# GpSimd's long pooling and splitting operations cut into short chains, in a fused pooled-attention and top-1 MoE kernel

## The chip, the core and the metric

The kernel runs on one core of a Trainium2 chip. The metric is device time in microseconds (us) of one execution, the median of several runs. Engines are named as the profile names them: PE (matmul) and PEld (weight load), DVE (VectorE), ACT (ScalarE), POOL (GpSimd), SP (the engine that issues most transfers).

## The reference

Attention over keys and values that are averaged in groups of 8, then a mixture of 8 experts in which each token uses one:

```python
k_p = k.reshape(B, H, Sp, pool, D).mean(axis=3)      # B, H, S, D = 8, 8, 576, 64; pool = 8
v_p = v.reshape(B, H, Sp, pool, D).mean(axis=3)
scores = scale * np.matmul(q, k_p.transpose(0, 1, 3, 2))
attn = exp(scores - max); attn = attn / sum(attn)
x = np.matmul(attn, v_p)                             # as 4608 rows of 512
expert_idx = np.argmax(x @ w_gate, axis=1)           # 8 experts
y = np.maximum(x @ w1[e], 0.0) @ w2[e]               # e: the row's expert; w1 512 x 1024, w2 1024 x 512
out = softmax(x @ w_gate)[expert_idx] * y
```

## The kernel before

Each engine's instructions stand in the order in which the Python code calls them (a manual schedule); waits between engines are put in by the framework, and each engine takes its own queue in order.

The first part, up to about 240 us, is attention and routing. Its work is cut into 36 units of 128 query rows; `u_pt`, `u_lo`, `u_pv` and `u_nrm` are the steps of one unit: transpose the probabilities on PE, split them into two halves of 16 bits (ACT line 482, DVE line 488), multiply with the pooled V (PE line 514), normalise on DVE (lines 543 to 554). Between them stand scores of later units (`g_s` on PE, `g_min` on DVE line 466, `g_exp` on ACT line 473) and small DVE steps of routing, called fillers, one or two at a time (lines 589 to 660). A Python table, `hooks`, hangs other work on places of the loop over units: `put(16, "q", pool_k, 6, 0)` runs part 0 of pooling K of batch 6 at the start of unit 16.

POOL's queue holds, in this order and mixed by those places:
- pooling (`pool`, lines 296 to 299) of K and V of batches 1 to 7, 14 in all, written k1, v1 up to k7, v7 here. A loaded K or V is a tile of 128 partitions by 5 chunks by 512 values. Three additions halve it: 1280 values to `t1`, 640 to `t2`, 320 to `kp` or `vp`. From batch 4 on the first addition is part 0 and stands in one unit, the other two are part 1 and stand in the next. `t1` and `t2` lie in the staging tile `st2[0]`, into which SP later loads the first half of expert 0's second weight (line 88);
- scatters of routed rows (`scatter`, line 649), 36 indirect transfers of one unit's rows each; `apart` (line 567) puts two memsets between some of them;
- splits of expert 0's weights (`wsplit` with "p" or "P", lines 109 and 110): five times a product and a difference of 1024 values per partition;
- the split of the first block of routed rows (`split_early`, lines 819 and 820), from which SP makes the transposed input of the experts (line 829).

PE takes kp and vp in `k_pe` (line 326) and `v_pe` (line 340); they stand in PE's queue at fixed units, k7 at 24 and v7 at 25. ACT writes the high half of a weight (line 101), DVE the low half of three of them in quarters (line 793, `lsplit`).

The second part, from about 240 us, is a loop over blocks of 256 rows through the experts. The lines of the change are not in it.

Of the kernel before, what the change touches and what calls it, by code (L numbers as in the profile page):

```python
# [13 lines left out]
OP = mybir.AluOpType  # L14
# [18 lines left out]
def kernel(  # L33
# [10 lines left out]
    nc = tc.nc  # L44
    B, H, S, D = q.shape
    N, Dm = out.shape
# [21 lines left out]
    def walloc(pool, s):  # L68
        W1[s] = [pool.tile([128, DC, F], F16, name=f"w1_{s}{h}") for h in range(2)]
        W2[s] = [pool.tile([128, FC, Dm], F16, name=f"w2_{s}{h}") for h in range(2)]  # L70
# [21 lines left out]
    def wsplit(s, i, what="hl"):  # L92
        if i < 4:
            src = st1[i // 2][:, i % 2, :]
            h, l = W1[s][0][:, i, :], W1[s][1][:, i, :]
        else:
            i -= 4
            src = st2[i // 2][:, 2 * (i % 2):2 * (i % 2) + 2, :]
            h, l = W2[s][0][:, 2 * i:2 * i + 2, :], W2[s][1][:, 2 * i:2 * i + 2, :]
        if "h" in what:  # L100
            nc.scalar.activation(h, src, AF.Copy, scale=SW)  # L101
        if "l" in what:
            nc.vector.scalar_tensor_tensor(l, src, SW, h, op0=OP.mult, op1=OP.subtract)
        if what in "pP":
            last_pool[:] = []
            t, sw = scratch[2 * (what == "P") + i % 2], swc[:, 0:1]
            if len(src.shape) == 3:
                t, sw = t.rearrange("p (c x) -> p c x", c=2), swc[:, :, None]
            nc.gpsimd.tensor_tensor(t, src, sw.to_broadcast(list(src.shape)), op=OP.mult)
            nc.gpsimd.tensor_tensor(l, t, h, op=OP.subtract)  # L110

    jp = st1[1].rearrange("p c x -> p (c x)")[:, 0:128].bitcast(I32)
    nc.gpsimd.iota(jp, pattern=[[1, 128]], base=0, channel_multiplier=-1)
# [48 lines left out]
    zf = consts.tile([128, 1], F32, name="zf")  # L162
    swc = consts.tile([128, 2], F32, name="swc")
# [24 lines left out]
    for e in range(E):  # L188
# [13 lines left out]
    xh = bd[2].rearrange("p (j a x) -> p j a x", j=2, a=2)  # L202
    ys = [x.rearrange("p h d -> p (h d)") for x in ql]
    xg, xg2 = (VB[i].rearrange("p y c s x -> p (y c s x)").bitcast(F32)[:, 0:2 * XW]
               .rearrange("p (j x) -> p j x", j=2) for i in (2, 0))
# [37 lines left out]
    for c in range(5):  # L243
        src = w_gate.rearrange("(h d) e -> d h e", d=D)[:, HS[c]:HS[c] + 3, :]
# [45 lines left out]
    t1 = st[:, 0:1280].rearrange("p (c x) -> p c x", c=5)  # L290
    t2 = st[:, 1280:1920].rearrange("p (c x) -> p c x", c=5)

    def pool(src, dst, what=(0, 1)):
        last_pool[:] = []
        if 0 in what:
            nc.gpsimd.tensor_tensor(t1, src[:, :, 0:4 * D], src[:, :, 4 * D:], op=OP.add)  # L296
        if 1 in what:
            nc.gpsimd.tensor_tensor(t2, t1[:, :, 0:2 * D], t1[:, :, 2 * D:], op=OP.add)
            nc.gpsimd.tensor_tensor(dst, t2[:, :, 0:D], t2[:, :, D:], op=OP.add)

    def pool_now(src, dst, part):
        p1 = pbig[:, 0:1280].rearrange("p (c x) -> p c x", c=5)
# [6 lines left out]
    def pool_k(b, part):  # L309
        if part == 0:  # L310
            KVS["kp", b] = work.tile([128, 5, D], F32, name="kp", bufs=2)
        pool(kv[(2 * b) % 3], KVS["kp", b], (part,))

    def pool_v(b, part):
        if part == 0:
            KVS["vp", b] = work.tile([128, 5, D], F32, name="vp", bufs=2)
        pool(kv[(2 * b + 1) % 3], KVS["vp", b], (part,))
# [374 lines left out]
    def pooled(n, b):  # L692
        KVS[n, b] = work.tile([128, 5, D], F32, name=n, bufs=2)
        return kv[(2 * b + (n == "vp")) % 3], KVS[n, b]
# [4 lines left out]
    src, kp = pooled("kp", 0)  # L699
# [11 lines left out]
    src, vp = pooled("vp", 0)  # L711
# [83 lines left out]
    for j, at in enumerate((12, 13, 18, 17, 26, 27, 23, 28)):  # L795
        put(at, "act2", wsplit, 0, j, "h")
    for j, at, what in ((0, 14, 'P'), (2, 20, 'P'), (5, 31, 'p'), (6, 26, 'p'), (7, 30, 'p')):
        put(at, "q", wsplit, 0, j, what)
# [16 lines left out]
        pass_ids(gB, iB, gA, iA)  # L815

    def split_early():
        x = xg[:, :, 0:Dm]
        nc.gpsimd.tensor_tensor(xh[:, :, 0], x, zf[:, :, None].to_broadcast([128, 2, Dm]), op=OP.add)
        nc.gpsimd.tensor_tensor(xh[:, :, 1], x, xh[:, :, 0], op=OP.subtract)  # L820

    def split_x(x=xg, h=xh):
        x = x[:, :, 0:Dm]
# [27 lines left out]
    def first_block():  # L851
        split_early()
        keep_ids()
        move_ids()
        take_ids()
# [262 lines left out]
    for j in range(2):  # L1118
        x, h = xg[:, j, 0:Dm], xh[:, j]
# [9 lines left out]
    with tc.If(nc.values_load(tab[0:1, 1:2], engines=[ENG.Activation, ENG.DVE, ENG.SP], min_val=0, max_val=1) > 0):  # L1129
        for j in range(8):  # L1130
            wsplit(1, j)
        for j in range(4):
            wload(2, (2 * j, 2 * j + 2))
# [114 lines left out]
```

## Time and profile before

| what | value |
|---|---|
| median of 3 runs | 688.49 us (687.96 to 693.12) |
| the profiled execution | 686.63 us |
| its span, first to last instruction | 684.7 us |
| mean granted clock of TensorE | 0.937 |
| PE, DVE, ACT, POOL busy | 87%, 52%, 42%, 41% of the span |
| attention and routing | up to about 240 us |

The profiled execution lies 1.86 us under the median and 1.93 us over its own span. Busy shares are means over both parts. A DVE or POOL instruction that has started and is held by the other engine counts as busy, so a long duration of a small instruction is a wait.

### The profile page before, as it was taken

What the parts mean: (1) busy time and instruction counts of PE and PEld (TensorE: products, weight loads), DVE (VectorE), ACT (ScalarE), POOL (GpSimd) and SP (SyncE); (2) the same over time, 40 slices, a digit from 0 to 9 for tenths busy, and PEclk for the clock granted to TensorE, in tenths of its full rate; (3) what the DMA queues carried; (4) which work ended last, traced back from release to release, by engine and by line L of the source; (5) the groups of instructions that cost most, each with busy time, mean ns of one, the idle gap of its engine ahead of it and who ended that gap; (6) DMA issues with size and microseconds to landing.
All of it is one profiled execution on the core that took longest, in us unless ns stands there. A gap on an engine that the chain in (4) does not pass through costs nothing. (4 is left out here: it accounts for less than half of the span.)

```text
span 684.7 us, 16103 instructions
## 1 busy us (share of the span) xinstructions
PE 595.1 (87%) x4637; PEld 428.9 (63%) x4638; DVE 356.3 (52%) x749; ACT 288.3 (42%) x634; POOL 278.8 (41%) x488
## 2 busy tenths in 40 slices
PE   6697898688768695999699999998999899999992
PEld 4586797577756453467375666674777566667751
DVE  4659988999897423522268286222451272122121
ACT  1375777567753023412357266222542272222221
POOL 5794759776485511021224325223132223021221
PEclk9998989999999797899799999999999989999997
DMA  8974968947648561831285884923174223320200
GB/s 241 295 220 102 267 216 230 290 126 188 212 115 283 168 151 47 290 93 44 81 276 169 245 261 116 349 75 94 42 279 123 57 60 95 77 61 31 61 31 13
DMA packets 104397, 105.65 MB, mean 154 GB/s; under 512 B 62502, under 2 KB 72742, under 8 KB 104360
## 3 DMA queue, kind: packets, MB, share of 16 engines
q1 hardware_dynamic: 97720, 85.46, 45.0%
q0 software_dynamic: 6640, 19.71, 8.0%
q8 instruction: 22, 0.36, 0.2%
q14 instruction: 15, 0.12, 0.1%
HBM read 71.77 MB, written 22.06 MB: 137 GB/s over the span
## 5 line engine op out<-in xcount | busy, mean ns | idle before, releaser
L962 PEld LDWEIGHTS <-bd 128*128 128x128 f16 x936 | 93.5, 101 | 129.9 <-issue 19.0
L1143 POOL TENSOR_TENSOR spacer<-ql,iG 1x1 f32<-1x1 f32 x44 | 19.5, 443 | 207.3 <-ACT ql L1139 206.4
L825 DVE TENSOR_TENSOR bd<-vb,bd 128x1024 f16<-128x1024 f32 x21 | 25.8, 1227 | 145.8 <-ACT bd L824 88.9
L473 ACT ACTIVATE p<-ps,nmx 128x72 f32<-128x72 f32 x288 | 68.7, 325 | 53.1 <-DVE nmx L466 50.4
L956 DVE SCALAR_TENSOR_TENSOR bd<-pp,bd 128x512 f16<-128x512 f32 x44 | 30.3, 691 | 94.6 <-ACT bd L952 88.7
L952 ACT ACTIVATE bd<-pp 128x512 f16<-128x512 f32 x44 | 26.2, 597 | 113.2 <-PE pp L895 63.7
L962 PE MATMUL po<-w,bd 128*128 128x512 f16 x264 | 62.9, 398 | 4.8 <-PEq L1187 4.8
L962 PE MATMUL po<-kv,bd 128*128 128x512 f16 x264 | 60.7, 388 | 3.9 <-ACT bd L952 2.5
L456 PE MATMUL ps<-bd,qT 128*128 128x144 f32 x256 | 51.5, 331 | 9.8 <-ACT p L473 8.4
L1144 POOL DMA_INDIRECT out_dram<-ql,iG x44 | 46.5, 1058 | 22.0 <-issue 20.6
L649 POOL DMA_INDIRECT x_by_expert<-XR,rpos x36 | 35.8, 993 | 42.0 <-DVE ri L543 9.7
L962 PE MATMUL pq<-w,bd 128*128 128x512 f16 x192 | 47.9, 410 | 5.4 <-ACT qt L101 3.9
L296 POOL TENSOR_TENSOR st<-kv 128x1280 f32<-128x1280 f32 x14 | 40.8, 2914 | 25.7 <-DMA kv<-in_k_dram 18.4
L893 PE MATMUL pp<-kv,w 128*128 128x256 f16 (+2 forms) x176 | 44.4, 264 | 5.6 <-issue 5.3
L962 PE MATMUL pq<-kv,bd 128*128 128x512 f16 x216 | 48.4, 379 | 0.2 <-ACT bd L952 0.2
L456 PEld LDWEIGHTS ps<-bd,qT 128*128 128x128 f32 x256 | 40.6, 218 | 12.2 <-ACT p L473 9.7
L514 PE MATMUL po<-vb,ph 128*128 128x146 f16 (+2 forms) x384 | 33.7, 237 | 15.3 <-DVE l L552 4.9
L893 PE MATMUL pp<-kv,qt 128*128 128x256 f16 (+2 forms) x176 | 44.6, 265 | 2.0 <-issue 2.0
L1139 ACT ACTIVATE ql<-po,gB 128x512 f32<-128x512 f32 x22 | 15.1, 685 | 73.1 <-PE L893 43.4
L894 PE MATMUL ps<-kv,qt 128*128 128x256 f16 (+2 forms) x176 | 43.9, 260 | 1.4 <-issue 1.4
L895 PE MATMUL pp<-kv,qt 128*128 128x256 f16 (+2 forms) x176 | 44.6, 265 | 0.0
L894 PE MATMUL pp<-kv,qt 128*128 128x256 f16 (+2 forms) x176 | 44.6, 265 | 0.0
(219 smaller groups left out, 1430.2 us busy)
## 6 DMA issues: line engine op xcount, KB each, us to landing
st<-in_moe_w_dram SPq DMA_DIRECT2D x32, 1024.0 KB
vb<-x_by_expert SPq DMA_DIRECT2D x17, 514.0 KB
kv<-in_k_dram SPq DMA_DIRECT2D x7, 1024.0 KB
kv<-in_v_dram SPq DMA_DIRECT2D x7, 1024.0 KB
qt<-in_q_dram SPq DMA_DIRECT2D x6, 1024.0 KB
qt<-in_q_dram SPq DMA_DIRECT2D x4, 512.0 KB
kv<-in_k_dram SPq DMA_DIRECT2D x8, 128.0 KB
kv<-in_k_dram SPq DMA_DIRECT2D x2, 512.0 KB
```

The source lines that it names most:

```text
L296: nc.gpsimd.tensor_tensor(t1, src[:, :, 0:4 * D], src[:, :, 4 * D:], op=OP.add)
L456: nc.tensor.matmul(ps[:, x * 2 * KP:(x + 1) * 2 * KP], t[:, h, :], BD[b % 3][:, :, h, :], start=True, stop=True)
L473: nc.scalar.activation(p[:, h * KP:(h + 1) * KP], ps[:, x * KP:(x + 1) * KP], AF.Exp, bias=nmx[:, x:x + 1], scale=-1.0)
L514: nc.tensor.matmul(po[:, half, cols], a[:, c * 128:(c + 1) * 128], VB[b % 3][:, y, c, sl, 0:CW], start=st, stop=False, skip_group_check=True)
L649: st = nc.gpsimd.indirect_dma_start(out=xs, out_offset=bass.IndirectOffsetOnAxis(ap=Z["pos"][:, u:u + 1], axis=0), in_=X[:, u, :], in_offs ...
L893: nc.tensor.matmul(dst, wh, xT[:, d, 0:n], start=(d == 0), stop=False)
L894: nc.tensor.matmul(dst, wh, xT[:, DC + d, 0:n], start=False, stop=False)
L895: nc.tensor.matmul(dst, wl, xT[:, d, 0:n], start=False, stop=(d == DC - 1))
L952: nc.scalar.activation(hT[0][:, 2 * k:2 * k + 2, :].rearrange("p f t -> p (f t)"), pH[k], AF.Relu)
L956: V.scalar_tensor_tensor(l, pH[k], 0.0, h, op0=OP.max, op1=OP.subtract)
L962: nc.tensor.matmul(y, hT[x][:, f, 128 * j:128 * j + 128], W2[s][z][:, f, :], start=(half == x == z == f == 0), stop=(half == z == 1 and f ...
L1144: st = nc.gpsimd.indirect_dma_start(out=out, out_offset=bass.IndirectOffsetOnAxis(ap=iG[:, j:j + 1], axis=0), in_=ys[j], in_offset=None, b ...
```

## The change

Three places are rewritten; what is computed stays the same, and nothing else moves.

- `pool`: the three additions run chunk by chunk. Five chains of three additions, of 256, 128 and 64 values, take the place of one chain of 1280, 640 and 320. Part 0 is now chunks 0 and 1, part 1 chunks 2 to 4.
- `wsplit` on POOL: product and difference alternate over four quarters of 256 values, in place of one pair of 1024.
- `split_early`: copy and difference alternate over four pieces of 256 values, in place of one pair of 1024.

```diff
@@ wsplit
-            nc.gpsimd.tensor_tensor(t, src, sw.to_broadcast(list(src.shape)), op=OP.mult)
-            nc.gpsimd.tensor_tensor(l, t, h, op=OP.subtract)
+            for x in range(4):
+                c = (slice(None), slice(256 * x, 256 * x + 256))
+                if len(src.shape) == 3:
+                    c = (slice(None), x // 2, slice(256 * (x % 2), 256 * (x % 2) + 256))
+                nc.gpsimd.tensor_tensor(t[c], src[c], swc[:, 0:1].to_broadcast([128, 256]), op=OP.mult)
+                nc.gpsimd.tensor_tensor(l[c], t[c], h[c], op=OP.subtract)
@@ pool
-        if 0 in what:
-            nc.gpsimd.tensor_tensor(t1, src[:, :, 0:4 * D], src[:, :, 4 * D:], op=OP.add)
-        if 1 in what:
-            nc.gpsimd.tensor_tensor(t2, t1[:, :, 0:2 * D], t1[:, :, 2 * D:], op=OP.add)
-            nc.gpsimd.tensor_tensor(dst, t2[:, :, 0:D], t2[:, :, D:], op=OP.add)
+        for c in ((0, 1), (2, 3, 4))[what[0]] if len(what) == 1 else range(5):
+            nc.gpsimd.tensor_tensor(t1[:, c], src[:, c, 0:4 * D], src[:, c, 4 * D:], op=OP.add)
+            nc.gpsimd.tensor_tensor(t2[:, c], t1[:, c, 0:2 * D], t1[:, c, 2 * D:], op=OP.add)
+            nc.gpsimd.tensor_tensor(dst[:, c], t2[:, c, 0:D], t2[:, c, D:], op=OP.add)
@@ split_early
-        x = xg[:, :, 0:Dm]
-        nc.gpsimd.tensor_tensor(xh[:, :, 0], x, zf[:, :, None].to_broadcast([128, 2, Dm]), op=OP.add)
-        nc.gpsimd.tensor_tensor(xh[:, :, 1], x, xh[:, :, 0], op=OP.subtract)
+        for j in range(2):
+            for c in (slice(0, Dm // 2), slice(Dm // 2, Dm)):
+                nc.gpsimd.tensor_tensor(xh[:, j, 0, c], xg[:, j, c], zf.to_broadcast([128, Dm // 2]), op=OP.add)
+                nc.gpsimd.tensor_tensor(xh[:, j, 1, c], xg[:, j, c], xh[:, j, 0, c], op=OP.subtract)
```

POOL's queue at v7, the last pooling, before the change (`kv_131` is the loaded V, `st_0_66` holds t1 and t2; in brackets the semaphores for which a row waits: DMAHW a load, DMASW an earlier scatter, Pool POOL itself):

```order
L296 TENSOR_TENSOR st_0_66<-kv_131 128x1280 [waits DMAHW3_49,DMAHW2_49]
L648 MEMSET spacer 1x1 [waits Pool_49]
L649 DMA x_by_expert<-XR,rpos 38016x514 [waits DMASW7_49]
L298 TENSOR_TENSOR st_0_66<-st_0_66 128x640 [waits Pool_49]
L299 TENSOR_TENSOR vp<-st_0_66 128x320 [waits Pool_49]
```

The same place after the change, from the first addition to the first chain behind the scatter:

```order
L300 TENSOR_TENSOR st_0_66<-kv_131 128x256 [waits DMAHW3_49]
L301 TENSOR_TENSOR st_0_66<-st_0_66 128x128 [waits Pool_49]
L302 TENSOR_TENSOR vp<-st_0_66 128x64 [waits Pool_49]
L300 TENSOR_TENSOR st_0_66<-kv_131 128x256
L301 TENSOR_TENSOR st_0_66<-st_0_66 128x128 [waits Pool_49]
L302 TENSOR_TENSOR vp<-st_0_66 128x64 [waits Pool_49]
L651 MEMSET spacer 1x1
L652 DMA x_by_expert<-XR,rpos 38016x514 [waits DMASW7_49]
L300 TENSOR_TENSOR st_0_66<-kv_131 128x256
```

Two whole chains now stand ahead of the scatter and three behind it; within a chain each addition waits for POOL's own semaphore, and the first addition of a chain does not.

POOL's queue at the last product and difference ahead of `split_early`, before the change (`kv_154` is scratch, `w_01_63` the weight's low half, `bd_161` the split rows, `vb_164` the loaded block):

```order
L109 TENSOR_TENSOR kv_154<-st_1_67,swc 128x1024
L842 UNCONDITIONAL_BRANCH
L110 TENSOR_TENSOR w_01_63<-kv_154,w_00_62 128x1024 [waits Activation_49,Pool_49]
L819 TENSOR_TENSOR bd_161<-vb_164,zf 128x2x512 [waits DMAHW4_49]
L820 TENSOR_TENSOR bd_161<-vb_164,bd_161 128x2x512 [waits Pool_49]
```

The same place after the change, from the last quarter of the weight on:

```order
L113 TENSOR_TENSOR kv_154<-st_1_67,swc 128x256
L114 TENSOR_TENSOR w_01_63<-kv_154,w_00_62 128x256 [waits Pool_49]
L823 TENSOR_TENSOR bd_161<-vb_164,zf 128x256 [waits DMAHW4_49]
L824 TENSOR_TENSOR bd_161<-vb_164,bd_161 128x256 [waits Pool_49]
L823 TENSOR_TENSOR bd_161<-vb_164,zf 128x256
L824 TENSOR_TENSOR bd_161<-vb_164,bd_161 128x256 [waits Pool_49]
```

A pair became four pairs, and in each the second waits for the first. The queues of PE, DVE, ACT and SP hold the same instructions in the same order as before.

## Rows read from the trace of the kernel before

**Rows 1.** The whole span in 40 equal slices of 17.1 us (section 2 of the page): busy tenths of DVE and POOL.

```profile
DVE  4659988999897423522268286222451272122121
POOL 5794759776485511021224325223132223021221
```

**Rows 2.** Busy time by stretch of the first part (us from the span's start); columns: length, PE, PEld, DVE, ACT, POOL busy with the number of instructions, granted clock, DMA share, GB/s; the last line sums.

```profile
21.20:62.50 41.30, 31.61 (x245) 28.46 (x245) 30.28 (x60) 24.34 (x84) 34.84 (x18) 0.91 0.80 221
62.50:162.40 99.90, 82.84 (x795) 73.60 (x794) 92.98 (x244) 65.69 (x214) 72.97 (x71) 0.90 0.74 213
162.40:202.60 40.20, 31.86 (x327) 28.87 (x327) 36.66 (x114) 28.91 (x91) 24.66 (x34) 0.96 0.60 160
202.60:238.80 36.20, 26.30 (x258) 20.77 (x257) 23.16 (x111) 8.17 (x26) 21.97 (x37) 0.87 0.71 225
sum 217.60, PE 172.61 PEld 151.71 DVE 183.08 ACT 127.11 POOL 154.44; mean PE 43.15 PEld 37.93 DVE 45.77 ACT 31.78 POOL 38.61
```

**Rows 3.** DVE's groups of instructions by form; columns: count, busy us, mean ns of one, idle time before them. Line 598 with 32 values stands in units up to 32, with 16 values behind them, where POOL has no pooling or splits left.

```profile
L598 DVE SCALAR_TENSOR_TENSOR req<-ra,down 128x32 f32<-128x32 f32 x8 | 7.2, 898 | 0.0
L598 DVE SCALAR_TENSOR_TENSOR req<-ra,down 128x16 f32<-128x16 f32 x2 | 0.3, 170 | 0.0
```

**Rows 4.** DVE in order of time (start, duration in us): the first, two in the middle and the last of 30 DVE instructions between 21 and 207 us that last over 0.2 us longer than the shortest of their form.

```profile
27.00 2.85 DVE L389 SCALAR_TENSOR_TENSOR vc<-u,vc 128x40 f16<-128x40 f32 x1
...
79.24 3.59 DVE L598 SCALAR_TENSOR_TENSOR req<-ra,down 128x32 f32<-128x32 f32 x1
...
91.23 1.39 DVE L389 SCALAR_TENSOR_TENSOR vc<-u,vc 128x40 f16<-128x40 f32 x1
...
204.86 1.91 DVE L638 TENSOR_SCALAR res<-res 128x4 f32<-128x4 f32 x1
```

**Rows 5.** POOL in order of time, at three of the four places of the rows above.

```profile
78.85 0.99 POOL L649 DMA_INDIRECT x_by_expert<-XR,rpos  x1 [0.16 <-issue]
79.87 2.91 POOL L296 TENSOR_TENSOR st<-kv 128x1280 f32<-128x1280 f32 x1
...
91.02 1.54 POOL L298 TENSOR_TENSOR st<-st 128x640 f32<-128x640 f32 x1
92.64 0.87 POOL L299 TENSOR_TENSOR kp<-st 128x320 f32<-128x320 f32 x1
...
204.62 2.12 POOL L110 TENSOR_TENSOR w<-kv,w 128x1024 f16<-128x1024 f32 x1
```

**Rows 6.** POOL in order of time: k1 and the start of v1.

```profile
21.23 2.88 POOL L296 TENSOR_TENSOR st<-kv 128x1280 f32<-128x1280 f32 x1 [10.89 <-DMA kv<-in_k_dram]
24.20 1.54 POOL L298 TENSOR_TENSOR st<-st 128x640 f32<-128x640 f32 x1
25.82 1.13 POOL L299 TENSOR_TENSOR kp<-st 128x320 f32<-128x320 f32 x1
26.91 2.89 POOL L296 TENSOR_TENSOR st<-kv 128x1280 f32<-128x1280 f32 x1
```

**Rows 7.** POOL's groups by form (columns as in rows 3): pooling and weight splits.

```profile
L296 POOL TENSOR_TENSOR st<-kv 128x1280 f32<-128x1280 f32 x14 | 40.8, 2914 | 25.7 <-DMA kv<-in_k_dram 18.4 <-DMA kv<-in_v_dram 7.0 <-issue 0.2
L298 POOL TENSOR_TENSOR st<-st 128x640 f32<-128x640 f32 x14 | 22.7, 1623 | 0.8
L299 POOL TENSOR_TENSOR kp<-st 128x320 f32<-128x320 f32 x7 | 6.4, 920 | 0.6
L109 POOL TENSOR_TENSOR kv<-st,swc 128x1024 f32<-128x1024 f32 x3 | 5.7, 1902 | 0.1
L110 POOL TENSOR_TENSOR w<-kv,w 128x1024 f16<-128x1024 f32 x3 | 6.4, 2148 | 0.2
```

**Rows 8.** POOL in order of time: two-value operations, the second of which waits for the first.

```profile
200.34 0.19 POOL L805 TENSOR_TENSOR iC<-vb,zi 128x2 int32<-128x2 int32 x1
200.62 0.20 POOL L809 TENSOR_TENSOR vb<-far,zi 128x2 int32<-128x2 int32 x1
```

**Rows 9.** POOL in order of time: two operations that DVE's instructions with two inputs in SBUF held up.

```profile
29.88 2.56 POOL L298 TENSOR_TENSOR st<-st 128x640 f32<-128x640 f32 x1
...
139.59 2.15 POOL L109 TENSOR_TENSOR st<-st,swc 128x1024 f32<-128x1024 f32 x1
```

**Rows 10.** POOL's waits from 21.3 to 162.4 us, k1 to v7: what it waited for, total us, times, longest. 10.9 of the first line lie ahead of k1; the lines left out hold 1.0 us without "issue".

```profile
POOL st L296 <- DMA kv<-in_k_dram: 18.4, 4, 10.9
POOL x_by_expert L649 <- DVE ri L545: 7.2, 1, 7.2
POOL st L296 <- DMA kv<-in_v_dram: 7.0, 2, 4.0
POOL x_by_expert L649 <- DVE L L554: 6.2, 1, 6.2
...
```

**Rows 11.** Four engines in order of time, around the end of v7: POOL's last addition, SP's load of the second weight, PE's first use of vp, ACT's first use of that weight; last, PE's first product with the first block's transposed rows.

```profile
161.45 0.86 POOL L299 TENSOR_TENSOR vp<-st 128x320 f32<-128x320 f32 x1
167.08 0.65 SPq L88 DMA_DIRECT2D st<-in_moe_w_dram  x1
168.93 0.38 PE L340 MATMUL pq<-ident,vp 128*128 128x128 f32 x2
179.49 1.06 ACT L101 ACTIVATE w<-st 128x1024 f16<-128x1024 f32 x1 [2.07 <-DMA st<-in_moe_w_dram]
...
212.48 0.27 PE L893 MATMUL ps<-kv,w 128*128 128x256 f16 x1
```

## The prediction

> **What bounds the kernel now.** I read the busy slices first. DVE is nearly full in the first part and POOL is its busiest there as well, while both are half idle behind it [rows 1]; the change touches the first part alone. By stretch, DVE is busy for 93.0 of the 99.9 us from 62.5 to 162.4 and for 36.7 of the next 40.2; POOL for 73.0 and 24.7 [rows 2]. So DVE sets the pace, and POOL looks as if it had room.
>
> Then I asked what DVE is busy with. A routing step of 32 values takes 898 ns, and the same step with half the values, where POOL has nothing long to do, 170 [rows 3]. In order of time one sees why: 30 of DVE's instructions in the first part last longer than the shortest of their form, 46 us too long in all [rows 4], and nearly all end within 0.1 us of the end of a POOL operation, or behind it by their own length. DVE's line 389 starts at 91.23 and ends at 92.62; POOL's addition of 640 ends at 92.56 and the next link of that chain starts at 92.64. Line 638 ends at 206.77, POOL's difference at 206.74. Line 598 at 79.24 starts under a scatter and comes free only after the addition behind it, at 82.8 [rows 4, 5]. These are instructions that read two SBUF inputs, or small copies. So DVE waits out one whole POOL operation, and is let in at the link between two of a chain.
>
> **What the change gives.** A POOL operation in a chain lasts at most about 0.7 us in place of 2.9. A DVE instruction that comes at any moment of a pooling waits on average the sum of the squares of the durations over twice their sum: before (2.9, 1.54, 0.86 us) 1.1 us, after (0.73, 0.46, 0.33, worked out next) 0.29. Since POOL is also at work for longer, I count one and a half times as many such waits: 46 x 0.26 x 1.5 = 18 us stay, so about 28 us of DVE time go. If DVE alone set the pace, most of that would be the gain.
>
> **What it costs POOL.** The three additions last 2.88, 1.54 and 0.86 us for 1280, 640 and 320 values [rows 6, 7], the last where nothing disturbs it [rows 11]. That is 2.1 ns for a value and 0.19 us for an operation, and two-value operations last 0.19 to 0.20, so the line holds at its short end [rows 8]. Between an operation and one that waits for it lie 0.08 us (24.20 less 21.23 + 2.88; 200.62 less 200.34 + 0.19 again); one that doesn't wait starts 0.04 before the end of the last (26.91 against 26.95) [rows 6, 8]. A chunk is then 0.73 + 0.08 + 0.46 + 0.08 + 0.33 - 0.04 = 1.64 to 1.66 us; I take 1.66. Five are 8.3 us; the old chain took 5.4 (2.97 + 1.62 + 0.82). That is **2.9 us more for each of 14 poolings, 41 us**. A split of 1.90 + 2.15 us [rows 7] becomes four pairs of (0.62 + 0.08 + 0.68 - 0.04), 5.4 us: 1.3 more for each of five, and the same for the first block's split, 8 us. Together 49 us on an engine that has 63 idle in the whole first part (154.4 busy of 217.6) [rows 2].
>
> **Where that lands.** POOL takes its queue in order, so its room counts only if it lies ahead of the thing that is needed. From k1's start at 21.2 to v7's end at 162.3 POOL waits for 28.9 us (7.5 + 7.2 + 7.0 + 6.2 + 1.0) [rows 10]; the other 112.2 are work. If POOL is late everywhere, none of these waits come back: the loads have landed and the rows to scatter are ready. Its work becomes 112.2 + 40.6 + 2 x 1.3 = 155.4. DVE's instructions in turn hold POOL up: a product that is 1.90 long alone took 2.15 behind one of them [rows 7, 9], 0.25 us, and some 14 of that size (lines 362 and 793) lie behind 62 us and ahead of v7; 3.5 us. So v7 ends at 21.2 + 155.4 + 3.5 = **180**, not 162.3. PE's transposes of it start at 168.9 before [rows 11]; the cover of 6.6 us is gone, and PE, with the scores, the products and their ACT and DVE steps queued behind line 340, is 11.3 us late there. The poolings ahead of it are late too, by less. All that DVE has won ahead of v7 is spent waiting for vp.
>
> Behind v7, ten units are left. Seven of the 30 DVE waits stand there, 11.3 us (the last in rows 4). Some 24 instructions of the kinds that wait remain there; POOL runs short operations in some 60% of that time, each holds DVE by half of 0.65 us: 24 x 0.6 x 0.33 = 5 us. So 6 us come back. ACT's wait of 2.1 us for the second weight [rows 11] goes, since the units come later and the load, I assume, not by as much; 2 us. POOL's own end: from v7 to 238.8 it is busy for 46.6 of 76.4 us [rows 2], some 51 with the short gaps at its scatters; 51 + 3 x 1.3 + 1.3 + 1 = 57 behind 180 is 237, so the last scatters are in time and cost nothing. `split_early` ends near 209, where the row behind it stands at 200 now [rows 8], and the first expert products take its transposes at 212.5 [rows 11], a few us later after the change; the cover is thin, and its loss would cost up to 3 us. SP's wait ahead of the second weight grows (the first addition of v7's last chunk must have left `st2[0]`), and the small moves of V behind it in SP's queue wait too; unit 27 needs them, which I cover with PE's own lateness.
>
> The second part runs no changed line: 0.
>
> **Sum.** +11.3 - 6 - 2 = +3.3 us. The profiled execution took 686.6, so 689.9 on its scale; the median of the runs lies 1.9 above it at 688.5, so **692**. The bounds: no hold-up of POOL by DVE (-3.5) and all 11.3 of the waits behind v7 gone (-5) give 683; twice the hold-up (+3.5), the second weight late (+4) and the first block late (+3) give 702.
>
> **Rivals.**
>
> *POOL keeps up, and the kernel is faster.* It holds if a chunk takes 1.50 us or less: then v7 ends at 21.2 + 112.2 + 70 x (1.50 - 1.08) + 2.6 + 3.5 = 169, where PE wants it, and DVE's 28 us count for the ahead-of-v7 units as well, for which PE's own busy time leaves 17 us in the second stretch and 8 in the third [rows 2]; I take 20, so 669. For it: POOL's idle tenths in the page. Against it: four durations on one line and the same link of 0.08 us at two sizes [rows 6, 8].
>
> *Slower: the second weight comes late.* Its load was issued at 167.1 and ACT could read it at 179.5, 12.4 us later [rows 11]. With v7 at 180 the load starts there. If it again takes 12.4, ACT's high half, with the probabilities of the next unit queued behind it on ACT, is 13 us late, and only the 5 to 6 us behind it come back: +7 to +8, 696. It decides from a landing time of about 8 us on. Against it: 1 MB of q was issued just ahead of it before, and need not be there. The same side is reached if DVE holds POOL for its full length: 14 x 0.45 + some 70 small steps x 0.17 [rows 3] = 18 us in place of 3.5, v7 at 195, 706. The Trainium skill (SBUF — State Buffer, Who interferes with whom) states this: the port pair of VectorE and GpSimd is an exclusive lock, and whoever comes second is blocked for the whole instruction of the first. The trace agrees for DVE behind POOL; in the other direction it shows 0.25 us.
>
> *The link lets DVE in no more than before.* If POOL's short operations followed each other too closely, DVE would wait for a chain of 1.6 us or more; nothing is won and POOL's 49 us stay, 700 to 710. Rows 4 and 5 at 92.6 speak against it.
>
> **Chances.** A measurement of this kernel tells a difference of 1% (6.9 us) from none. Forecast, POOL full and v7 late with the end about where it was: 0.57. POOL keeps up: 0.08. Late weight or full hold-up: 0.28. No entry for DVE: 0.07. The range runs from 683 to 704: it reaches past the late weight and into the full hold-up and the closed link; beyond it lie the faster rival (0.08) and their upper ends (some 0.1).
>
> **What the profile after must show.** POOL busy near 330 us, not 279, and nearly without waits from 21 to 235. Additions of 0.73, 0.46 and 0.33 us, chunks 1.66 apart. The step of 32 values on DVE at 300 to 450 ns, not 898, and no DVE wait above 1.8 us, a scatter and the addition behind it. PE waiting for POOL's vp, the last time near 180. Wrong would be: POOL idle for more than 20 us in the first part (the step on the chunk's price failed), or DVE's waits as long as before (the step on the links).

## The result and the profile after

The kernel takes **692.2 us** (median of 20 runs, 687.4 to 697.0), the kernel before 688.1 (median of 20 runs): the ratio is 1.0068, with a 95% interval from 1.0042 to 1.0093. The ratios, here and below, leave out executions over 1.5% above the fastest of their kernel in the same comparison; the medians are of all. So the change costs 4 us: the interval doesn't reach down to 1, though the difference is under the 1% of the forecast's bound. The profiled execution took 697.0 us, the longest of these 20, and its span is 694.9; the one of the kernel before took 686.6, span 684.7. Not all of the 10 us between the two profiles belong to the change, therefore: the first part ends 4.3 us later, about the difference of the medians (4.1), and the rest lies in the second part, whose code is the same (below).

Busy time by engine, whole span, and the slices of DVE and POOL (sections 1 and 2 of the page of the kernel after):

```profile
PE 595.5 (86%) x4637; PEld 429.5 (62%) x4638; DVE 322.5 (46%) x749; ACT 288.5 (42%) x634; POOL 316.5 (46%) x692
...
DVE  4566868548676523512366375322362281122121
...
POOL 5899889899877611022226411323223223112221
```

The four stretches of [rows 2] (length; PE, PEld, DVE, ACT, POOL busy with the number of instructions; granted clock; DMA share; GB/s):

```profile
21.20:62.50 41.30, 30.24 (x221) 26.88 (x221) 21.57 (x53) 22.73 (x79) 37.77 (x68) 0.88 0.70 209
62.50:162.40 99.90, 81.68 (x825) 72.86 (x824) 72.35 (x254) 67.33 (x221) 90.19 (x175) 0.93 0.71 210
162.40:202.60 40.20, 32.70 (x309) 28.65 (x307) 32.35 (x108) 27.55 (x87) 33.18 (x62) 0.87 0.59 170
202.60:238.80 36.20, 26.98 (x269) 22.92 (x267) 20.79 (x102) 9.51 (x31) 25.08 (x52) 0.86 0.64 203
```

The two engines have changed places, in the slices [rows 1] and in the stretches. Between 62.5 and 162.4 us DVE was busy for 93.0 of 99.9 us and is now for 72.4; POOL went from 73.0 to 90.2 [rows 2], and what it lacks to 99.9 is mostly the gap at each link. PE, which all this serves, has gained little: its busy time there has hardly moved (82.8 to 81.7), and 825 of its matmuls are recorded there where 795 were.

DVE's step of 32 values, against [rows 3] (count, busy us, mean ns):

```profile
L601 DVE SCALAR_TENSOR_TENSOR req<-ra,down 128x32 f32<-128x32 f32 x8 | 2.7, 339 | 0.0
```

The step has gone from 898 ns to 339; that of 16 values, where POOL has nothing long, is at 170 as before. Summed as for [rows 4] (all that is over 0.2 us longer than the shortest of its form), DVE's waits between 21 and 215 us are 34 with 15 us in all, where they were 30 with 46.

POOL's groups of the poolings, against [rows 7] (last column: idle just ahead of them):

```profile
L300 POOL TENSOR_TENSOR st<-kv 128x256 f32<-128x256 f32 x70 | 54.8, 783 | 9.0 <-DMA kv<-in_k_dram 8.7
...
L301 POOL TENSOR_TENSOR st<-st 128x128 f32<-128x128 f32 x70 | 32.4, 463 | 5.5
...
L302 POOL TENSOR_TENSOR kp<-st 128x64 f32<-128x64 f32 x35 | 12.4, 355 | 2.7
L302 POOL TENSOR_TENSOR vp<-st 128x64 f32<-128x64 f32 x35 | 11.5, 328 | 2.7
```

The additions took 40.8 + 22.7 us, 6.4 for K's last ones [rows 7] and 7.9 for V's, 78 in all. They now take 111.1 (54.8 + 32.4 + 12.4 + 11.5), and 10.9 us more are idle ahead of the second and third of a chain (5.5 + 2.7 + 2.7), 0.08 us for each of 140 links.

POOL's waits from 21.3 us to the end of v7, against [rows 10] (total us, times, longest):

```profile
POOL x_by_expert L652 <- issue: 2.4, 15, 0.2
POOL x_by_expert L652 <- DVE XR L550: 0.2, 1, 0.2
```

Of 28.9 us of waiting, counted without "issue" as there, 0.2 are left. The loads that POOL waited for have long landed, and the rows that it scatters are ready: up to the end of v7 POOL is late everywhere.

The end of v7, against [rows 11]: POOL's last addition; SP's load of the second weight; PE's transposes of vp and what each waited for; ACT's first use of the weight; PE's first product with the first block's rows, each from its engine's list in order of time (start, duration):

```profile
174.89 0.32 POOL L302 TENSOR_TENSOR vp<-st 128x64 f32<-128x64 f32 x1
...
175.24 0.37 SPq L88 DMA_DIRECT2D st<-in_moe_w_dram  x1
...
173.65 0.47 PE L343 MATMUL pq<-ident,vp 128*128 128x128 f32 x1 [4.15 <-POOL vp L302]
175.26 0.42 PE L345 MATMUL pq<-ident,vp 128*64 128x128 f32 x1 [1.14 <-POOL vp L302]
...
183.42 1.07 ACT L101 ACTIVATE w<-st 128x1024 f16<-128x1024 f32 x1
...
214.42 0.27 PE L897 MATMUL ps<-kv,w 128*128 128x256 f16 x1
```

v7 ends at 175.2 in place of 162.3, and PE, which had it lying ready before, waits 4.15 and 1.14 us for it. How often PE waits for POOL in the whole stretch from 21 to 203 us:

```profile
PE pq L343 <- POOL vp L302: 16.5, 5, 4.1
PE pq L345 <- POOL vp L302: 4.2, 5, 1.1
...
PE pq L329 <- POOL kp L302: 1.3, 1, 1.3
```

22 us; in the kernel before there is no such wait. This is the new wait that DVE's gain went into.

### The profile page after: what moved, and what is told of

Its sections match the earlier page's. It is cut to its first block, busy times and chain, and to the rows that moved or that the text cites. A ratio compares the mean times of both kernels' runs of the same rounds, so it can differ in the third digit from the quotient of the medians.

```text
span 694.9 us, 16295 instructions
## 1 busy us (share of the span) xinstructions
PE 595.5 (86%) x4637; PEld 429.5 (62%) x4638; DVE 322.5 (46%) x749; ACT 288.5 (42%) x634; POOL 316.5 (46%) x692
## 5 line engine op out<-in xcount | busy, mean ns | idle before, releaser
L966 PE MATMUL po<-w,bd 128*128 128x512 f16 x264 | 66.1, 412 | 9.3 <-ACT bd L956 5.4
L300 POOL TENSOR_TENSOR st<-kv 128x256 f32<-128x256 f32 x70 | 54.8, 783 | 9.0 <-DMA kv<-in_k_dram 8.7
L1148 POOL DMA_INDIRECT out_dram<-ql,iG x44 | 44.9, 1021 | 22.0 <-issue 20.6
L966 PE MATMUL pq<-w,bd 128*128 128x512 f16 x192 | 45.4, 393 | 7.9 <-ACT qt L101 3.6
L1146 POOL TENSOR_TENSOR iG<-iB,zi 128x1 int32<-128x1 int32 (+1 forms) x44 | 9.3, 210 | 79.8 <-DMA out_dram<-ql,iG 71.9
L898 PE MATMUL ps<-kv,qt 128*128 128x256 f16 (+2 forms) x176 | 43.9, 260 | 1.4 <-issue 1.4
L897 PE MATMUL ps<-kv,qt 128*128 128x256 f16 (+2 forms) x176 | 43.9, 260 | 0.3 <-issue 0.2
```

What stands on the lines that cost most here:

```text
L300: nc.gpsimd.tensor_tensor(t1[:, c], src[:, c, 0:4 * D], src[:, c, 4 * D:], op=OP.add)
L897: nc.tensor.matmul(dst, wh, xT[:, d, 0:n], start=(d == 0), stop=False)
L898: nc.tensor.matmul(dst, wh, xT[:, DC + d, 0:n], start=False, stop=False)
L966: nc.tensor.matmul(y, hT[x][:, f, 128 * j:128 * j + 128], W2[s][z][:, f, :], start=(half == x == z == f == 0), stop=(half == z == 1 and f ...
L1148: st = nc.gpsimd.indirect_dma_start(out=out, out_offset=bass.IndirectOffsetOnAxis(ap=iG[:, j:j + 1], axis=0), in_=ys[j], in_offset=None, b ...
```

## The experiments

**Which part of the change costs?** The first two runs take it apart.

Poolings alone as chains:

```diff
@@ wsplit, split_early: as in the kernel before
@@ pool: as in the change
```

> The poolings as chains of chunks; the weight splits and the first block's split long, as before. Theory (POOL full ahead of v7, DVE's gain is spent waiting for vp): two of the five weight splits lie ahead of v7, so v7 ends 2.6 us earlier than with the whole change, 172 to 173; behind it DVE waits again for whole splits, some 3 us. Together 690 to 693, as the whole change (692). Rival (the loss comes behind v7, from the splits and the late first block): 688 or less, as the kernel before.

Measured: 692.2 us, ratio to before 1.0087 (1.0046 to 1.0127), as the whole change. v7 ends at 171.65, just below the 172 to 173 expected, and PE waits 16 us for POOL (10.0 + 3.6 + 2.5).

The splits alone:

```diff
@@ pool: as in the kernel before
@@ wsplit, split_early: as in the change
```

> Only the weight splits and the first block's split as chains; poolings long, as before. Theory: POOL gets 2.6 us more ahead of v7, which the 6.6 us ahead of PE's use of it cover; DVE's waits behind v7 (11 us in the kernel before) fall to some 5. So 682 to 686, faster than before. Rival (the splits are what costs): 690 to 693.

Measured: 686.5 us, just above the 682 to 686 expected, ratio 0.986 (0.978 to 0.994). The six executions lie from 676 to 692, and the ratio rests on two of them, so how much the splits gain by themselves, if anything, is not settled; no loss shows. The poolings alone cost what the whole change costs, so the loss is theirs, and the split chains, the rival, do no harm on the whole.

**Is it POOL's total, or the many operations?** Two chains keep POOL's load low, three lie between, and one more operation a chunk raises it.

```diff
-        for c in ((0, 1), (2, 3, 4))[what[0]] if len(what) == 1 else range(5):
+        for c in [(slice(0, 2), slice(2, 5))[x] for x in what]:
```

> Each pooling as two chains of three operations (two chunks: 512, 256, 128 values; three chunks: 768, 384, 192), 6.1 us in place of 8.2 with five chains and 5.4 with one; the splits as in the whole change. Theory: v7 ends between 160 and 166, where PE is not yet waiting for it; DVE waits some 25 us in all, not 46 nor 15. So 674 to 682, faster than both kernels. Rival (POOL's load ahead of v7 is not what costs): as the whole change, 690 to 693.

Measured: **673.4 us, ratio 0.978** (0.973 to 0.983), faster than both kernels and just under the 674 to 682 expected. v7's last addition there, and POOL's waits up to it:

```profile
155.44 0.59 POOL L302 TENSOR_TENSOR vp<-st 128x192 f32<-128x192 f32 x1
```

```profile
POOL x_by_expert L652 <- DVE ri L548: 4.7, 1, 4.7
POOL x_by_expert L652 <- DVE L L557: 3.8, 1, 3.8
POOL st L300 <- DMA kv<-in_k_dram: 2.2, 1, 2.2
```

v7 ends at 156 (160 to 166 was expected), PE doesn't wait for POOL, and POOL itself waits again, for a load and for rows that DVE has yet to write, a sign that it has room. DVE's waits sum to 22 us, more than the 15 of five chains, less than 46.

The same stretches as above, for two chains:

```profile
62.50:162.40 99.90, 85.98 (x867) 78.45 (x867) 86.92 (x272) 72.22 (x237) 84.03 (x116) 0.93 0.80 239
162.40:202.60 40.20, 34.13 (x344) 29.91 (x343) 32.59 (x115) 26.53 (x87) 32.81 (x62) 0.92 0.64 192
```

Now PE does more in the stretch (86.0 us and 867 matmuls, where the kernels before and after have 795 and 825), and DVE's busy time is up with it: it has more units to serve.

```diff
-            for c in [(slice(0, 2), slice(2, 5))[x] for x in what]:
+            for c in [x for i in what for x in ((slice(0, 2),), (slice(2, 4), slice(4, 5)))[i]]:
```

> Each pooling as three chains of three operations (two, two and one chunk). By the line of 0.19 us an operation and 2.1 ns a value with links of 0.08 us that is 6.8 us on POOL, 0.7 more than two chains and 1.4 less than five. Theory: v7 ends some 10 us later than with two chains (156), near 165, about where PE comes to want it, and DVE's waits are a few us shorter than the 21 there; so little beyond the two-chain time, 673 to 681, and far from the 692 of five. Rival (the number of operations sets the time in proportion: 6, 9, 15 a pooling at 673, x, 692): 679 to 681 as the midpoint, and PE waiting for vp already.

Measured: 674.9 us, ratio 0.979 (0.975 to 0.984): with two, three and five chains the time is 673, 675 and 692. It doesn't grow with the number of operations, it turns where POOL runs out of room. v7 ends at 159 there, 6 us ahead of what was expected, so three chains are still on the flat side.

```diff
             nc.gpsimd.tensor_tensor(dst[:, c], t2[:, c, 0:D], t2[:, c, D:], op=OP.add)
+            nc.gpsimd.tensor_tensor(st[:, 1920:1984], dst[:, c], zf.to_broadcast([128, D]), op=OP.add)
```

> The whole change, and one more operation of 64 values behind each chunk, fed by its result, into a spare place that nobody reads: 0.33 + 0.08 = 0.41 us, 70 times, 29 us. Theory (POOL is full from k1 to v7): v7 ends 27 to 29 us later, near 203, and the kernel takes 20 to 28 us more, 712 to 720. Rival (POOL still has slack there): 692 to 698.

Measured: 718.5 us, ratio 1.045 (1.041 to 1.050), 26 us over the whole change. v7's end:

```profile
199.40 0.32 POOL L302 TENSOR_TENSOR vp<-st 128x64 f32<-128x64 f32 x1
```

PE waits for vp for 44 us (32.5 + 11.1). v7 ends 24.5 us later, where 27 to 29 was expected, and the kernel takes 26 more: on this side of the turn nearly every microsecond of POOL comes back in the time.

**Does DVE get in at every end of an operation, or only where the next one waits?** The same 15 operations in another order tell:

```diff
-            nc.gpsimd.tensor_tensor(t1[:, c], src[:, c, 0:4 * D], src[:, c, 4 * D:], op=OP.add)
-            nc.gpsimd.tensor_tensor(t2[:, c], t1[:, c, 0:2 * D], t1[:, c, 2 * D:], op=OP.add)
-            nc.gpsimd.tensor_tensor(dst[:, c], t2[:, c, 0:D], t2[:, c, D:], op=OP.add)
+            nc.gpsimd.tensor_tensor(t1[:, c], src[:, c, 0:4 * D], src[:, c, 4 * D:], op=OP.add)
+        for c in C:
+            nc.gpsimd.tensor_tensor(t2[:, c], t1[:, c, 0:2 * D], t1[:, c, 2 * D:], op=OP.add)
+        for c in C:
+            nc.gpsimd.tensor_tensor(dst[:, c], t2[:, c, 0:D], t2[:, c, D:], op=OP.add)
```

> Poolings in the same 15 short operations, but level by level: the additions of 256 of a part's chunks, then those of 128, then those of 64; none is fed by the one just ahead of it, but for one at each turn of level. The splits as in the whole change. Nine or ten gaps of 0.08 us become overlaps of 0.04, so POOL saves 1.0 to 1.2 us for a pooling, and v7 ends near 161. If DVE is let in only where a POOL operation waits for the one ahead of it, DVE waits for whole levels, up to 2.2 us, and step of 32 values takes 0.7 to 1.2 us: 686 to 692. If it is let in at the end of any operation, that step stays near 0.35 us and the time is 674 to 681.

Measured: 685.6 us, ratio 0.993 (0.989 to 0.997), just under the 686 to 692 of the first case. The step of 32 values takes 794 ns in the mean, as that case has it. v7 ends at 169 and not near 161, since POOL itself stands 9.1 us ahead of a scatter, whose rows DVE writes late. DVE's waits sum to 38 us, with operations as short as in the change. The longest, in order of time on DVE, and POOL in the same microseconds (x3: three operations in a row on one line):

```profile
140.88 6.15 DVE L598 TENSOR_TENSOR ra<-L,rm 128x32 f32<-128x32 f32 x1
```

```profile
139.53 2.08 POOL L301 TENSOR_TENSOR st<-kv 128x256 f32<-128x256 f32 x3
141.58 1.26 POOL L303 TENSOR_TENSOR st<-st 128x128 f32<-128x128 f32 x3
...
145.82 0.58 POOL L305 TENSOR_TENSOR kp<-st 128x64 f32<-128x64 f32 x2
146.37 0.60 POOL L113 TENSOR_TENSOR st<-st,swc 128x256 f32<-128x256 f32 x1
147.05 0.67 POOL L114 TENSOR_TENSOR w<-st,w 128x256 f16<-128x256 f32 x1
```

A step of 32 values sees the ends of 14 short operations go by and is let in at 146.97, where the product of a split ends and the difference behind it has to wait for it: a link. None of the operations ahead is longer than 0.75 us. So short operations by themselves don't let DVE in at each end. I had expected a link at each turn of level, too, and so waits up to 2.2 us; the rows show none, since 141.58 stands ahead of 139.53 + 2.08: the result that the new level needs is two operations old.

The link is not the only place, though. Of the 19 DVE waits over 0.5 us in this run, 13 end where one addition follows another without a gap. In one, DVE's line 395 comes free at 94.42, in the middle of three additions of 128:

```profile
93.02 1.40 DVE L395 SCALAR_TENSOR_TENSOR vc<-u,vc 128x40 f16<-128x40 f32 x1
```

```profile
93.48 1.27 POOL L303 TENSOR_TENSOR st<-st 128x128 f32<-128x128 f32 x3
```

What decides at which of these ends DVE gets in, the runs don't show. At a link it always did: of the 432 DVE waits over 0.2 us that begin between 21 and 215 us in the 13 profiles of this document, none goes on past a gap of 0.05 us or more in POOL's work.

**Does the gain of short chains appear once POOL is relieved in another way?** The third addition goes to DVE, as one instruction of 320 values; t2 gets a second buffer for it.

```diff
+    t2 = [st[:, 768 + 640 * i:1408 + 640 * i].rearrange("p (c x) -> p c x", c=5) for i in range(2)]
-            nc.gpsimd.tensor_tensor(dst[:, c], t2[:, c, 0:D], t2[:, c, D:], op=OP.add)
+    def pool_last(dst, t2):
+        nc.vector.tensor_tensor(dst, t2[:, :, 0:D], t2[:, :, D:], op=OP.add)
@@ k_pe, v_pe, ahead of the transposes
+        if b:
+            pool_last(kp, t2[0])
```

> The whole change with its five chains, but the third addition of each pooling is one instruction of 320 values on DVE, ahead of PE's transposes. A chunk on POOL is 0.73 + 0.08 + 0.46 - 0.04 = 1.23 us, a pooling 6.2 in place of 8.2: POOL has 28 us less, as much as with two chains, and its operations stay short. DVE gets 14 instructions of some 0.55 us, 8 us. Theory (POOL's load ahead of v7 is what eats the gain): v7's additions on POOL end between 150 and 160, time 672 to 681. Rival (it is the many short operations themselves that cost, not POOL's total): 692 to 700.

> Two chains for each pooling, of two operations each on POOL (512, 256; 768, 384), the third addition on DVE: 4.9 us on POOL for a pooling, less than the 5.4 of the kernel before. DVE's waits lie as with two chains, 20 to 25 us, and its own work is 8 us more. If POOL's load still sets the pace at two chains (6.1 us), this is faster than they were (673): 664 to 670. If DVE and PE do by then, it is no faster: 672 to 682.

In both, K of sequence 2 is taken from sequence 3's second additions, and v7 from a weight that was loaded over them, so their times carry a wait that isn't meant. Measured: 680.3 us with five chains (0.990, 0.987 to 0.993), 688.1 with two (0.998, 0.993 to 1.003). The first is 12 us under the whole change, as the theory says. Of the time that DVE stands ahead of its additions of vp, 8.7 us are the weight's landing. The second was expected at 664 to 682 and missed it on the slow side. Its profiled execution, 677.9, was the fastest of its 12, and doesn't show where the others lose 10 us; this stays open.

```diff
@@ prep
+        if b > 1:
+            put(k[0] - 1, "dve2", last_of, "kp", b)
+        put(v[0] - 1, "dve2", last_of, "vp", b)
```

> Five chains of two operations on POOL, the third addition on DVE as in the earlier run, but put at the end of the unit ahead of PE's transposes and not directly ahead of them (and so in the right order for sequence 2, whose K the earlier run took from sequence 3). POOL's load and the short holds of DVE are those of the earlier run (680). If its 17 us of PE waiting for DVE's kp and vp are what kept it above two chains, they go and it takes 670 to 677. If DVE merely waits there itself for POOL, with its queue behind it, it stays at 678 to 683.

Measured: 678.8 us, ratio 0.984 (0.978 to 0.990), the second case: PE's waits for kp and vp fell from 17 us to 3, but DVE stood there instead, with 8.3 us of the weight's landing ahead of v7's addition, which still adds the weight.

```diff
-            put(k[0] - 1, "dve2", last_of, "kp", b)
-        put(v[0] - 1, "dve2", last_of, "vp", b)
+            put(k[0] - 1, "dve", last_of, "kp", b)
+        put(v[0] - 1, "dve", last_of, "vp", b)
```

> As the run before, five chains of two operations on POOL and the third addition on DVE one unit ahead of PE's use; now v7's stands ahead of the load of the second weight in the program. In the two earlier runs with five chains that load stood ahead of it, took its input's place, and DVE waited 8.3 to 8.7 us for the load to land before it added (and added the weight). POOL's load is 2.0 us a pooling lighter than in the whole change, 28 in all. Theory: v7 is pooled near 160, DVE's waits stay at 10 to 12 us, and the 8 us of the load's landing go from 679 to 680: 668 to 675, well under the whole change (692) with chains as short. Rival (many short operations cost by themselves): 685 or more.

Measured: 665.9 us where the kernel before took 679.4 in the same comparison, ratio 0.981 (0.976 to 0.986). At the 688 of the kernel before, that is 675, the upper end of what was expected and well under 692. v7 is pooled at 158, near the 160 expected; DVE's waits are 17 us and not 10 to 12. With chains as short as in the change, and 28 us less on POOL, DVE's gain is there.

**Last, the split chains where POOL has room:** two chains with the splits long.

```diff
@@ pool: two chains, as above
@@ wsplit, split_early: as in the kernel before
```

> Two chains for each pooling; the weight splits and the first block's split long as in the kernel before. Theory: the split chains cost nothing ahead of v7 once POOL has room, and spare DVE 4 to 7 us of waits behind it; without them 677 to 681. If the split chains give nothing: 671 to 675.

Measured: 677.5 us, ratio 0.985 (0.978 to 0.991), against 0.978 (0.973 to 0.983) with split chains. The medians differ by the 4 us expected, but the intervals overlap, and three of the six executions lie at 673 to 674, as with split chains, three at 681 to 685; it is not settled.

## Why the prediction was right, and where two of its terms were not

**DVE's waits.** I expected 18 us of 46 to stay; 15 did. The longest wait is the one that I had set as the limit, a scatter and the operation behind it: DVE's line 616 comes free at 188.89, 1.4 us late, and what is queued behind it as well.

```profile
186.87 1.01 POOL L652 DMA_INDIRECT x_by_expert<-XR,rpos  x1
187.89 0.97 POOL L212 MEMSET vb<- 128x1028 f32 x1
```

```profile
187.35 1.54 DVE L616 COPY XR<-ids 128x4 int32<-128x4 int32 x1
```

**A chunk's price.** Expected 0.73, 0.46 and 0.33 us and 1.66 from chunk to chunk. The first part of k1:

```profile
21.14 0.73 POOL L300 TENSOR_TENSOR st<-kv 128x256 f32<-128x256 f32 x1
21.95 0.46 POOL L301 TENSOR_TENSOR st<-st 128x128 f32<-128x128 f32 x1
22.48 0.32 POOL L302 TENSOR_TENSOR kp<-st 128x64 f32<-128x64 f32 x1
22.77 0.72 POOL L300 TENSOR_TENSOR st<-kv 128x256 f32<-128x256 f32 x1
```

1.63. The line through three durations held, down to a fifth of the smallest one that it came from. The total of 49 us held as well, but I named it wrongly: POOL's *busy* time was to be near 330 and is 316.5. The links are idle time, and 10.9 us of the 49 are links; 37.7 more busy and 10.9 idle make 48.6. Taken literally, one sign of being wrong did come: POOL idle for more than 20 us in the first part. It is busy for 186.2 of the 217.6 us (37.8 + 90.2 + 33.2 + 25.1) and idle for 31. But the step that this sign was to test, the chunk's price, held. Of the idle time 14.6 us lie ahead of the end of v7, none of it over 0.3 us at a time; behind v7 POOL does wait again, 11 us for rows that DVE writes, where the forecast had it nearly without waits.

**v7's end and PE.** Expected 180, measured 175.2. Three terms were a little large: the chunks (70 x 0.03 = 2 us); k1's first addition, which now needs one chunk's rows and not all five and starts at 19.36, not 21.2; and DVE's hold on POOL, which grew by 2.4 us (from 3.8 to 6.2, all that is over 0.1 us longer than usual for its form), not 3.5. PE's last wait for vp ends at 175.26; the same transposes stood at 169.14 before, so PE is 6.1 us late there and not 11.3.

That DVE's gain came first and was then spent shows at the units. DVE's line that writes `pl` marks them, counted from 0; units 20 and 21 of the kernel before, and of the kernel after:

```profile
146.44 0.83 DVE L488 SCALAR_TENSOR_TENSOR pl<-pp,ph 128x640 f16<-128x640 f32 x1
...
151.91 0.81 DVE L488 SCALAR_TENSOR_TENSOR pl<-pp,ph 128x640 f16<-128x640 f32 x1
```

```profile
140.20 0.82 DVE L491 SCALAR_TENSOR_TENSOR pl<-pp,ph 128x640 f16<-128x640 f32 x1
...
152.76 0.81 DVE L491 SCALAR_TENSOR_TENSOR pl<-pp,ph 128x640 f16<-128x640 f32 x1
```

The kernel after is 6.2 us ahead at unit 20 and 0.9 behind at unit 21: between them PE waits 6.6 us for v6 (2.57 + 2.90 + 1.14). With v7 it loses 5 more.

**Behind v7.** Here I expected DVE's and ACT's shorter waits to give back 8 us. Units 26, 33 and 34 of the kernel before, and of the kernel after:

```profile
175.14 0.81 DVE L488 SCALAR_TENSOR_TENSOR pl<-pp,ph 128x640 f16<-128x640 f32 x1
...
214.99 0.82 DVE L488 SCALAR_TENSOR_TENSOR pl<-pp,ph 128x640 f16<-128x640 f32 x1
...
218.15 0.81 DVE L488 SCALAR_TENSOR_TENSOR pl<-pp,ph 128x640 f16<-128x640 f32 x1
```

```profile
181.25 0.82 DVE L491 SCALAR_TENSOR_TENSOR pl<-pp,ph 128x640 f16<-128x640 f32 x1 [0.58 <-issue]
...
215.41 0.82 DVE L491 SCALAR_TENSOR_TENSOR pl<-pp,ph 128x640 f16<-128x640 f32 x1 [0.20 <-ACT ph L485]
...
222.65 0.82 DVE L491 SCALAR_TENSOR_TENSOR pl<-pp,ph 128x640 f16<-128x640 f32 x1 [0.85 <-ACT ph L485]
```

The lateness is 6.1 us at unit 26 and 0.4 at unit 33: 5.7 us do come back. At unit 34 it is 4.5 again. The forecast put 3 us at most there, for a late first block. PE's first product with that block stands at 214.42, 1.9 later than before [rows 11], but it waits for nothing there; what ACT and DVE wait for between 216 and 222 the profile doesn't name ("remote", 5.7 and 1.7 us). The other runs show what this loss goes with. From unit 33 to unit 35 it takes 6.3 us in the kernel before and in both runs with long splits; 11.5 in the change, 11.5 with two chains, where v7 is early, and 8.7 to 11.5 in the other runs with split chains. So it comes with the split chains and not with the late v7; how, stays open. What comes back goes with them as well: from unit 26 to unit 33 it takes 41.1 us with the poolings alone and 34.2 in the change, 36.9 with two chains and long splits and 32.9 with two chains and split ones (39.9 before).

The end of the first part, the table of blocks on DVE, of before and of after:

```profile
L1062 DVE CAST tabs<-pq x1: 195/195/195, 239.3 to 239.3; 7x48 int32<-7x48 f32 x1
```

```profile
L1066 DVE CAST tabs<-pq x1: 197/197/197, 243.6 to 243.6; 7x48 int32<-7x48 f32 x1
```

+4.3 us, where the sum said +3.3. So the sum came out by two errors that cancel: 5 us too much ahead of v7, and 6 too much given back behind it (8 expected, 6.1 less 4.3 = 2 measured). That the forecast hit 692 to the microsecond is luck; that POOL would be full ahead of v7, with vp late and DVE's gain spent on it, is what the runs with less and with more work on POOL bear out.

**The second part.** Expected 0. The profiled executions differ there by 5.9 us (694.9 less 243.6, 684.7 less 239.3). In the profiles of the experiments it took from 441 to 451 us, in no relation to the shape of the first part, and the medians differ by no more than the first part does. I count it as the spread of single runs.

**The rivals.** The late weight didn't come: its load was issued at 175.24, ACT used it at 183.42 and waited for nothing, so it landed in 8.2 us at most, where [rows 11] had shown 12.4. A hold of DVE on POOL for the full length of each instruction didn't come at the size that I gave it: 6.2 us in all, not 18. The 70 small steps, 12 of the 18 us, held no operation of POOL by over 0.1 us; the long instructions did (last section). POOL doesn't keep up at a chunk of 1.63 us; but the price of that rival, 669, was sound, as two and three chains show with 673 and 675.

## What to carry to other kernels

An engine that blocks another is worth cutting into pieces only as long as its queue has room ahead of the thing that is needed next: count what a pooling costs in the new shape, add it up along that queue, and choose the coarsest pieces that still let the other engine in. Here two pieces gave 2.2%, five lost 0.7%. And put a link behind each piece, an operation that waits for the one ahead of it: there the other engine was always let in. Among pieces that follow each other without one it was let in at some ends and not at others, and in the run by levels DVE's waits were 38 us where chains of the same short operations left 15.

## What the runs showed of the hardware that I had not expected

Short POOL operations without links between them can hold DVE as one: 6 us past the ends of 14 operations of at most 0.75 us, in the run by levels above. They don't always, as the rows at 93.48 there show. The forecast had seen this at two operations, a scatter and an addition.

DVE's hold on POOL depends on the length of DVE's instruction. In the kernel after, two instructions of DVE's line 409, 1.3 us each, lie over these two operations of POOL, which take 0.32 and 0.73 elsewhere:

```profile
27.49 2.59 DVE L409 TENSOR_TENSOR vb<-vc,mk 128x1080 f16<-128x1080 f16 x2
```

```profile
27.60 1.35 POOL L302 TENSOR_TENSOR kp<-st 128x64 f32<-128x64 f32 x1
28.91 1.76 POOL L300 TENSOR_TENSOR st<-kv 128x256 f32<-128x256 f32 x1
```

They are held by 1.03 us each. The second takes 0.73 us alone and ends 0.59 behind the end of DVE's second instruction (30.08): it had got hardly anything done until then. Line 365, 0.5 us long, holds POOL by 0.25 us at most. The Trainium skill (SBUF — State Buffer, Who interferes with whom) says that whoever comes second is blocked for the whole instruction of the first; for the long instructions these rows agree. The forecast took 0.25 us from one row of [rows 9] and missed what the other shows: the addition of 640 at 29.88, 1.54 us long elsewhere, takes 2.56 there, a hold of 1.0 us before the change already.
